# Attention scores from three 32-row terms per head, or from one 64-row and one 32-row matmul

## The chip, the cores and the metric

The kernel runs on one core of a Trainium2 chip. A core has five engines with queues of their own: TensorE (PE in the profile, with its weight loads listed as PEld), VectorE (DVE), ScalarE (ACT), GpSimd (POOL) and SyncE (SP), which here issues nearly all DMAs. Matmuls write to PSUM; the program uses it in banks of 128 x 512 float32. The metric is the device time of one execution in microseconds, and the number compared is the median of several runs.

## The reference

One transformer block with adaptive layer norm on 2048 tokens of width 448, in float32:

```python
mod = (silu(c) @ w_mod).reshape(1, 6, 1, -1)
sa, ca, ga, sb, cb, gb = (mod[:, i] for i in range(6))
h = layernorm(x) * (1 + ca) + sa
x = x + ga * A(h)          # softmax attention, 16 heads of 28, then @ wo
h = layernorm(x) * (1 + cb) + sb
x = x + gb * B(h)          # layernorm, 448 -> 1792, gelu, 1792 -> 448

# inside A, for each head
scores = einsum("bhqd,bhkd->bhqk", q, k) * 28 ** -0.5
p = softmax(scores)
o = einsum("bhqk,bhkd->bhqd", p, v)
```

The weights are drawn large, so that the scores are large too and the softmax needs the maximum of each row and scores of nearly float32 precision.

## The kernel before

**Precision.** Most matmuls run on `fp32r` operands. A value is split into a rounded part, hi, and the rest, lo, and a product is the sum of hi by hi, hi by lo and lo by hi. For scores this means three matmuls: K's hi by Q's hi, K's lo by Q's hi, K's hi by Q's lo.

**Stages.** In phase 1 (to about 181 us in the profiled execution) the kernel makes the first layer norm, Q, K and V for four blocks of 512 tokens, and some of the row maxima. `qk_task` (L336) makes four heads of Q or K for one block, in 128 rows: each head has 32, of which 28 are data. K has a one in row 28 of each head, and row 28 of Q's hi later gets minus the row maximum, so that the matmul subtracts it. `split` (L356) writes the hi and the lo part to DRAM, in `dscr[kind][part][g]`, for later. Attention follows (181 to 859 us), and then the MLP to the end at 1154 us. The MLP's weights are prepared in the last steps of attention.

**The attention loop** (L1017 to L1057) has 16 units, g by qt: four groups of four heads, by four blocks of 512 queries. A unit has 16 steps, one per 128 keys. A step makes the scores of four heads for 128 keys and 512 queries in two halves `hf` of two heads each. One half has a PSUM tile `s` of two banks (two such tiles take turns), filled by six matmuls: three terms by two heads, each on the 32 rows of its head (L1037 to L1040). Half 0 uses rows 0 to 63, half 1 rows 64 to 127. ScalarE takes the exponent of the half's 128 x 1024 scores (L1045) into `pt`. Behind the two halves stands PV of the step before (`av`, L1007): one matmul per head, 128 keys to 32 output rows, which the trace records as two passes each. In this text PV is the name of that block.

**The maxima.** The row maxima that group g + 1 needs are taken during group g, from hi parts alone. `max_one` (L395) is a 32-row matmul into one of three `mx` banks, followed by a reduction on VectorE (L397). `n_maxima` (L999) gives each step three or four, in turn, and few to those steps that also carry output projections; `emit_max` (L487) picks from the list of open maxima one whose head `j` suits the place: while half 0 computes, heads 2 and 3 (the other 64 rows), and heads 0 and 1 while half 1 does. TensorE works in the order in which the loop writes it, so a maximum that waits for its bank holds what is written behind it.

**Loads.** `load_q` (L571) reads the hi and lo of one unit's queries into slot `b0` or `b1`, in turn, as one tile of 128 x 2 x 512; `load_k` (L568) reads 512 keys into `a0` to `a3`. `load_hi` (L416) reads hi parts for the maxima. `max_fin` (L424) puts minus the maxima into Q's rows 28 of each head, in one DMA. `load_o` (L747) brings back staged attention outputs for the output projection (`t_wo`, L795). All these go through SP's queue in the order written. Slots are shared over the stages: the tags in `halved` (L67) are kept as two separate tiles of half the size, so that their halves can be used by different things.

The core of the score loop, before:

```python
for hf in range(2):
    s2 = ps_s2()
    for term, (kp, qp) in enumerate(((0, 0), (1, 0), (0, 1))):
        for jj in range(2):
            rows_ = slice(64 * hf + 32 * jj, 64 * hf + 32 * jj + 32)
            pe.matmul(s2[:, jj, :], ks[rows_, kp, kc], qs[rows_, qp, :], ...)
```

Of the kernel before, what the change touches and what calls it, by code (L numbers as in the profile page):

```python
# [14 lines left out]
F32R = mybir.dt.float32r  # L15
# [6 lines left out]
S = 2048  # L22
D = 448
H = 16
DH = 28
# [3 lines left out]
NB = S // 512  # L29
NG = H // 4  # L30
# [11 lines left out]
def tile_adaln_block(ctx: ExitStack, tc: tile.TileContext, x, wqkv, wo, w1, b1, w2, b2, c, w_mod, out):  # L42
    nc = tc.nc
    pe, act, dve, pool, sp = nc.tensor, nc.scalar, nc.vector, nc.gpsimd, nc.sync
# [6 lines left out]
    dr = ctx.enter_context(tc.tile_pool(name="dr", bufs=1, space=DRAM))  # L51
# [4 lines left out]
    def nm(t):  # L56
        uid[0] += 1
        return f"{t}_{uid[0]}"

    def sbt(tag, shape, dt=F32, bufs=1):  # L60
        return sb.tile(shape, dt, tag=tag, name=nm(tag), bufs=bufs)

    def slot(tag, shape, dt=F32R):
        return sb.tile(shape, dt, tag="slot_" + tag, name=nm("slot_" + tag), bufs=1)


    halved = ("a2", "a3", "b1")  # L67

    def slot4(tag, inner):
        if tag not in halved:  # L70
# [5 lines left out]
    def ps_s2():  # L76
        return psp[0].tile([128, 2, 512], F32, tag="s", name=nm("s"), bufs=psp[2])
# [4 lines left out]
    def ps_mx():  # L82
        return psp[0].tile([128, 512], F32, tag="mx", name=nm("mx"), bufs=psp[1])
# [7 lines left out]
    def f(t):  # L91
        return t.bitcast(F32)
# [184 lines left out]
    for k in range(NC):  # L277
        for j in range(2):
            pe.matmul(
                pm[32 * j : 32 * j + 32, :D], sil_b[:, k, :], wm_ac[k // 2][:, k % 2, j * D : (j + 1) * D],  # L280
                start=(k == 0), stop=(k == NC - 1),
# [21 lines left out]
    def v_init(i):  # L303
# [2 lines left out]


    dscr = [
        [[dr.tile([128, S], F32R, tag=f"d{kind}{part}{g}", name=f"d{kind}{part}{g}", bufs=1) for g in range(NG)] for part in range(2)]
        for kind in range(2)  # L310
    ]
    kh_sb = {}
# [16 lines left out]
    def qk_terms(b, kind, g):  # L329
        ts = terms448(  # L330
            *hT[b],
            lambda k: wq[kind][0](k)[:, 4 * g : 4 * g + 4, :], lambda k: wq[kind][1](k)[:, 4 * g : 4 * g + 4, :],
        )
        return ps_s(), [(w, h) for h, w in ts]

    def qk_task(b, kind, g, done=0, begun=None):  # L336
        p, ts = begun or qk_terms(b, kind, g)
        for i in range(done, len(ts)):
            pe.matmul(p, *ts[i], start=(i == 0), stop=(i == len(ts) - 1))  # L339
        emit_task(*p1_n)  # L340
        bias = ones_col if kind == 1 else zero_col
        if g == 0:
            tg = ("kh" if kind else "qh") + str(b)
            hi = sb.tile([128, 512], F32R, tag=tg, name=nm(tg), bufs=1)
            (kh_sb if kind else qh_sb)[(g, b)] = hi
        elif g == 1 and b < 2:

            hi = sbt("raw" if kind else "osb", [128, 512], F32R, bufs=3 if kind else 2)
            (kh_sb if kind else qh_sb)[(g, b)] = hi
        else:  # L350
            hi = sbt("hi", [128, 512], F32R, bufs=3)
        full = sbt("full", [128, 512], bufs=3)
        lo = sbt("lo", [128, 512], F32R, bufs=3)
        act.activation(full, p, AF.Identity, bias=bias)

        def split():  # L356
            (act.copy if b else dve.tensor_copy)(hi, full)
            if kind == 1 and (g, b) == (0, 1):
                k_diff.append(sbt("raw", [128, 512], F32R, bufs=3))
                pool.tensor_tensor(out=k_diff[0], in0=f(hi), in1=f(kh_sb[(0, 0)]), op=ALU.subtract)  # L360
            pool.tensor_tensor(out=lo, in0=full, in1=f(hi), op=ALU.subtract)
            sl = slice(b * 512, (b + 1) * 512)
            sp.dma_start(f(dscr[kind][0][g])[:, sl], f(hi))
            sp.dma_start(f(dscr[kind][1][g])[:, sl], f(lo))

        return split

# [13 lines left out]
    mxq = []  # L381
# [13 lines left out]
    def max_one(g, qt, cch, i, j, ps=None):  # L395
        m = max_mm(g, qt, i, j, kh_sb[(g, cch)], ps)
        dve.tensor_reduce(out=mxp[(g, qt)][:, i, j, cch : cch + 1], in_=m, op=ALU.max, axis=AX.X)  # L397
# [18 lines left out]
    def load_hi(kind, g, b):  # L416
        tg = ("kh" if kind else "qh") + str(b)
        t = sb.tile([128, 512], F32R, tag=tg, name=nm(tg), bufs=1)
        (kh_sb if kind else qh_sb)[(g, b)] = t
        sp.dma_start(f(t), f(dscr[kind][0][g])[:, b * 512 : (b + 1) * 512])  # L420

    late = []

    def max_fin(g, qt):  # L424
        m16 = sbt("m16", [128, 4, 4], bufs=2)
        c0 = 1 if (g, qt) in paired else 0
        dve.tensor_reduce(out=m16, in_=mxp[(g, qt)][:, :, :, c0:].rearrange("p i h c -> p h i c"), op=ALU.max, axis=AX.X)

        def put():
            p = ps_mx()  # L430
            pe.transpose(p[:16, :128], m16.rearrange("p h i -> p (h i)"), ident)
            r = sbt("full", [128, 512], F32R, bufs=3)[:16, :128]
            act.activation(r, p[:16, :128], AF.Copy, scale=-1.0)  # L433
            sp.dma_start(f(qst[g * NB + qt])[DH:128:32, 0, :].rearrange("j (i q) -> j i q", q=128), f(r))

        late.append([2, put, g * NB + qt])

# [47 lines left out]
    last_j = [None]  # L485

    def emit_max(n, half=None):  # L487
        for _ in range(n):
            if not mxq:
                return  # L490
            fits = [x for x, m in enumerate(mxq[:32]) if half is None or (m[4] // 2 == half and m[4] != last_j[0])]
            g, qt, cch, i, j = mxq.pop(fits[0] if fits else 0)
            last_j[0] = j
            max_one(g, qt, cch, i, j)
            count(g, qt, [cch])
# [27 lines left out]
    def finish_max(g, qt):  # L523
        while left[(g, qt)] > 0:
            emit_max(1)
# [33 lines left out]
    kst = {}  # L559
    qst = {}  # L560

    def load_parts(tag, kind, g, sl):
        t = slot(tag, [128, 2, 512])
        for part in range(2):
            sp.dma_start(f(t)[:, part, :], f(dscr[kind][part][g])[:, sl])
        return t

    def load_k(g, ch):  # L568
        kst[(g, ch)] = load_parts(f"a{ch}", 1, g, slice(ch * 512, (ch + 1) * 512))

    def load_q(u):  # L571
        g, qt = divmod(u, NB)
        qst[u] = load_parts(f"b{u % 2}", 0, g, slice(qt * 512, (qt + 1) * 512))

    b1_col = sbt("b1_col", [128, NFT])

# [167 lines left out]
    def last_g(qt):  # L744
        return NG - 2 if qt == NB - 1 else NG - 1

    def load_o(qt):  # L747
        for g, tag in zip(range(last_g(qt)), ("a2h", "a3h", "b1h")):
            t = slot(tag, [128, 2, 512])
            for part in range(2):  # L750
                sp.dma_start(f(t)[:, part, :], f(doh[part][g])[:, qt * 512 : (qt + 1) * 512])
            o_in[(qt, g)] = t
# [210 lines left out]
    q0, q1 = f"b{(NU - 2) % 2}", f"b{(NU - 1) % 2}"  # L963
# [53 lines left out]
    for u in range(NU):  # L1017
        g, qt = divmod(u, NB)
        for kt in range(NKT):
            step = u * NKT + kt  # L1020
            if kt == 1 and u + 1 < NU and u + 1 not in qst:
                load_q(u + 1)
            if kt == NKT - 6 and u + 1 < NU:
                finish_max(*divmod(u + 1, NB))
            tick_late()
            if not (three or mxq or late):
                three = True
                share(1, 3)
            pt = slot(ptags[step % 3], [128, 4, 512], F32)
            n = n_maxima(step)  # L1030
            n0 = 1 if n == 3 and step % 4 == 3 else 2

            ks, qs = kst[(g, kt // 4)], qst[u]
            kc = slice((kt % 4) * 128, (kt % 4 + 1) * 128)
            for hf in range(2):
                s2 = ps_s2()
                for term, (kp, qp) in enumerate(((0, 0), (1, 0), (0, 1))):  # L1037
                    for jj in range(2):
                        rows_ = slice(64 * hf + 32 * jj, 64 * hf + 32 * jj + 32)
                        pe.matmul(s2[:, jj, :], ks[rows_, kp, kc], qs[rows_, qp, :], start=(term == 0), stop=(term == 2))  # L1040
                    if hf == 0 and term < min(n0, n):
                        emit_max(1, 1)
                    if hf == 1 and ((term == 0 and n - n0 > 0) or (term == 2 and n - n0 > 1)):
                        emit_max(1, 0)
                act.activation(pt[:, 2 * hf : 2 * hf + 2, :], s2, AF.Exp, scale=SCALE)  # L1045
            if pend is not None:
                pu, pkt, pp, po = pend
                av(pu, pkt, pp, po)
                if pkt == NKT - 1:
                    end_unit(pu, po)  # L1050
            if kt == 0:
                o = ps_o()
            pend = (u, kt, pt, o)
            if qt == NB - 1 and kt % 4 == 3 and g + 1 < NG:
                load_k(g + 1, kt // 4)
            for fn in sched.pop(step, ()):
                fn()  # L1057
# [50 lines left out]
    for n in range(len(seq) + LAG):  # L1108
        if n < len(seq):
            b, i = seq[n]  # L1110
# [37 lines left out]
```

## Time and profile before

| | |
|---|---|
| median of three runs | 1153.68 us (1153.37 to 1156.09) |
| profiled execution, its time | 1156.12 us |
| profiled execution, its span | 1154.1 us |
| granted TensorE clock, mean | 0.997 |
| attention, first score matmul to last PV | 181.2 to about 859 us |
| a unit of attention (first twelve), PV to PV | 39.7 to 41.5 us |
| score matmuls (L1040) | 3072, mean 425 ns |
| maxima's matmuls (L392, `mx` from `kh`, `qh`) | 899, mean 471 ns |
| their reductions (L397) | 919, mean 684 ns |
| exponents (L1045) | 512, mean 1022 ns |
| PV matmuls (L1010) | 2048 in two passes each, mean 608 ns |

In the profile, a matmul's line gives its start, its duration and how many are merged in the line. Durations of matmuls overlap: the next one starts while the one before still has its tail, and matmuls on different rows of the array start together. What a matmul costs is therefore read from the distance between starts. An idle time in brackets is followed by what ended it.

### The profile page before, as it was taken

The page shows a single profiled execution, that of the slowest core. Times are in us where ns is not written, and L with a number is a line of the kernel's source. Part 1 is how long each engine was busy: PE and PEld are TensorE (multiplying, and loading weights), DVE is VectorE, ACT ScalarE, POOL GpSimd, SP SyncE. Part 2 cuts the span into 40 slices and gives each one's busy share as a digit, 9 for nine tenths or more (in the row PEclk, how much of TensorE's full clock was granted, in tenths as well). Part 3 has the DMA queues.
Part 4 walks back from the last instruction along what each step waited for, and adds up shares of the span by engine and source line. Part 5 has one row for each costly group of instructions (what it writes and reads, how often), then busy time and mean ns, then how long its engine had stood idle before and what let it go on. Part 6 is the DMA issues. An engine that isn't in the chain of part 4 may idle for free. (4 is left out here: it accounts for less than half of the span.)

```text
span 1154.1 us, 20722 instructions
## 1 busy us (share of the span) xinstructions
PE 1142.3 (99%) x8396; PEld 685.5 (59%) x8396; DVE 827.6 (72%) x1471; ACT 685.0 (59%) x855; POOL 215.0 (19%) x216
## 2 busy tenths in 40 slices
PE   8999999999999999999999999999999999999998
PEld 6767765444444444444444445555458888888887
DVE  6868787999888889889888976585448863444322
ACT  4666756877777787777777877675862221111110
POOL 2534431210000000000000011206213513213000
PEclk9999998999999999999999999999999999999999
DMA  8653354121132111321110321120323100000000
GB/s 299 206 145 114 100 193 119 38 65 57 31 96 79 57 38 38 88 71 55 50 57 29 83 84 44 41 78 8 110 69 90 48 33 1 1 32 1 32 1 32
DMA packets 50415, 81.07 MB, mean 70 GB/s; under 512 B 11512, under 2 KB 20812, under 8 KB 50320
## 3 DMA queue, kind: packets, MB, share of 16 engines
q1 hardware_dynamic: 49696, 79.01, 21.8%
q8 instruction: 66, 1.08, 0.4%
q10 hardware_dynamic: 288, 0.46, 0.1%
q0 software_dynamic: 336, 0.28, 0.1%
q14 instruction: 29, 0.24, 0.1%
HBM read 53.11 MB, written 26.35 MB: 69 GB/s over the span
## 5 line engine op out<-in xcount | busy, mean ns | idle before, releaser
L397 DVE TENSOR_REDUCE mxp<-mx 128x1 f32<-128x512 f32 x919 | 580.0, 684 | 112.8 <-PE mx L392 107.8
L1040 PE MATMUL s<-slot_b,slot_a 32*128 32x512 f32 x3072 | 384.1, 425 | 1.6 <-ACT full L433 0.7
L1045 ACT ACTIVATE slot_c<-s 128x1024 f32<-128x1024 f32 x342 | 331.7, 1022 | 87.4 <-PE s L1040 83.4
L1040 PEld LDWEIGHTS s<-slot_b,slot_a 32*128 32x128 f32 x3072 | 217.4, 184 | 239.7 <-ACT slot_c L1045 138.8
L392 PE MATMUL mx<-kh,qh 32*128 32x512 f32 x899 | 293.8, 471 | 0.4
L1045 ACT ACTIVATE slot_d<-s 128x1024 f32<-128x1024 f32 x170 | 164.8, 1021 | 44.7 <-PE s L1040 44.6
L1010 PE MATMUL o<-slot_c,v 128*32 128x512 f32 x1368 | 184.2, 608 | 0.4 <-ACT osb L979 0.4
L1081 ACT ACTIVATE full<-mx,b_col 128x512 f32<-128x512 f32 x56 | 38.5, 688 | 191.9 <-PE mx L317 179.8
L392 PEld LDWEIGHTS mx<-kh,qh 32*128 32x128 f32 x899 | 118.4, 182 | 13.3 <-DVE mxp L397 7.8
L1084 DVE CAST hi<-full 128x512 fp32r<-128x512 f32 x56 | 25.2, 450 | 135.0 <-ACT full L1081 135.0
L778 POOL TENSOR_TENSOR osb<-osb,osb 128x512 f32<-128x512 f32 x16 | 20.9, 1305 | 491.4 <-DMA osb<-drec 251.1
L1010 PE MATMUL o<-slot_d,v 128*32 128x512 f32 x680 | 90.6, 605 | 0.0
L1010 PEld LDWEIGHTS o<-slot_c,v 128*32 128x32 f32 x1368 | 27.2, 108 | 56.7 <-issue 52.0
L317 PE MATMUL mx<-y,slot_a 128*128 128x512 f32 x160 | 60.6, 395 | 0.0
L405 ACT ACTIVATE slot_d<-mx 128x512 f32<-128x512 f32 x48 | 27.0, 597 | 40.5 <-PE mx L392 40.3
L1085 DVE TENSOR_TENSOR lo<-full,hi 128x512 fp32r<-128x512 f32 x56 | 44.1, 788 | 5.6 <-DVE hi L1084 0.5
L317 PE MATMUL mx<-y,slot_c 128*128 128x512 f32 x152 | 47.5, 396 | 0.1
L1099 PE MATMUL s<-slot_v,lo 128*128 128x448 f32 x128 | 46.7, 365 | 0.0
L1097 PE MATMUL s<-slot_v,hi 128*128 128x448 f32 x128 | 46.6, 364 | 0.0
L317 PE MATMUL mx<-y,slot_v 128*128 128x512 f32 x112 | 39.2, 396 | 0.0
L317 PE MATMUL mx<-y,slot_b 128*128 128x512 f32 x112 | 39.0, 397 | 0.0
L339 PE MATMUL pa<-slot_c,slot_a 128*128 128x512 f32 x136 | 36.9, 405 | 0.0
(224 smaller groups left out, 1392.1 us busy)
## 6 DMA issues: line engine op xcount, KB each, us to landing
d<-lo SPq DMA_DIRECT2D x32, 256.0 KB
slot_b<-d SPq DMA_DIRECT2D x32, 256.0 KB
slot_a<-d SPq DMA_DIRECT2D x32, 256.0 KB
d<-hi SPq DMA_DIRECT2D x20, 256.0 KB
osb<-drec SPq DMA_DIRECT2D x15, 256.0 KB
out_dram<-xn SPq DMA_DIRECT2D x16, 224.0 KB
slot_v<-in_w_mod_dram SPq DMA_DIRECT2D x4, 784.0 KB
raw<-in_B_w_dram SPq DMA_DIRECT2D x14, 224.0 KB
```

Of the source, the lines that this page charges most:

```text
L317: pe.matmul(p, a, b, start=(i == 0), stop=(i == len(terms) - 1))
L339: pe.matmul(p, *ts[i], start=(i == 0), stop=(i == len(ts) - 1))
L392: pe.matmul(m, qh_sb[(g, qt)][js, i * 128 : (i + 1) * 128], k[js, :], start=True, stop=True)
L397: dve.tensor_reduce(out=mxp[(g, qt)][:, i, j, cch : cch + 1], in_=m, op=ALU.max, axis=AX.X)
L405: act.activation(r, m, AF.Relu)
L1010: pe.matmul(o[32 * j : 32 * j + 32, :], v_sb[kt // 4][:, kt % 4, 4 * g + j, :], p[:, j, :], start=(kt == 0), stop=(kt == NKT - 1),)
L1040: pe.matmul(s2[:, jj, :], ks[rows_, kp, kc], qs[rows_, qp, :], start=(term == 0), stop=(term == 2))
L1045: act.activation(pt[:, 2 * hf : 2 * hf + 2, :], s2, AF.Exp, scale=SCALE)
L1081: act.activation(gf, p, AF.Gelu_apprx_tanh, bias=b1_col[:, i : i + 1])
L1085: dve.tensor_tensor(out=glo, in0=gf, in1=f(ghi), op=ALU.subtract)
L1097: pe.matmul(pp, ghi[:, ts], w_hi, start=(m == 0), stop=False)
L1099: pe.matmul(pp, glo[:, ts], w_hi, start=False, stop=(m == NFT - 1))
```

## The change

Per half of a step, the six 32-row matmuls become four: two of 64 rows and two of 32. K's tile now holds, for each head, hi and lo one above the other in 64 rows, and Q's tile `q1` holds Q's hi twice, so one 64-row matmul gives K's hi by Q's hi plus K's lo by Q's hi. A second tile `q2` has Q's lo twice; a 32-row matmul adds K's hi by Q's lo. In each half the two heads now sit in rows 0 to 63 and 64 to 127. For half 0, K's hi lies in the upper 32 rows of each 64, for half 1 in the lower 32, so the 32-row matmuls of half 0 use row groups 0 and 2 and those of half 1 use row groups 1 and 3. The maxima of a half are written behind its four matmuls, and use the heads on the row groups that the 32-row matmuls leave free: odd heads in half 0, even heads in half 1. Their number per half stays.

To load the tiles in this form, K is stored with hi and lo exchanged for the lower 64 rows, in two DMAs where there was one, and is loaded in four DMAs for two; Q is loaded in six for two; K's hi for the maxima in two for one; minus the maxima are put in two for one. The tags `a1` and `b0` become halved, `q2` lives in `b0h` or `b1h`, and the third staged output moves from `b1h` to `a1h`.

```diff
-    halved = ("a2", "a3", "b1")
+    halved = ("a1", "a2", "a3", "b0", "b1")
...
     dscr = [
-        [[dr.tile([128, S], F32R, tag=f"d{kind}{part}{g}", name=f"d{kind}{part}{g}", bufs=1) for g in range(NG)] for part in range(2)]
+        [dr.tile([2, 128, S], F32R, tag=f"d{kind}{g}", name=f"d{kind}{g}", bufs=1) for g in range(NG)]
         for kind in range(2)
     ]
...
-            sp.dma_start(f(dscr[kind][0][g])[:, sl], f(hi))
-            sp.dma_start(f(dscr[kind][1][g])[:, sl], f(lo))
+            for part, src in enumerate((hi, lo)):
+                if kind == 0:
+                    sp.dma_start(f(dscr[0][g])[part, :, sl], f(src))
+                else:
+                    sp.dma_start(f(dscr[1][g])[part, 0:64, sl], f(src)[0:64])
+                    sp.dma_start(f(dscr[1][g])[1 - part, 64:128, sl], f(src)[64:128])
...
-        sp.dma_start(f(t), f(dscr[kind][0][g])[:, b * 512 : (b + 1) * 512])
+        sl = slice(b * 512, (b + 1) * 512)
+        if kind == 0:
+            sp.dma_start(f(t), f(dscr[0][g])[0, :, sl])
+        else:
+            sp.dma_start(f(t)[0:64], f(dscr[1][g])[0, 0:64, sl])
+            sp.dma_start(f(t)[64:128], f(dscr[1][g])[1, 64:128, sl])
...
-            sp.dma_start(f(qst[g * NB + qt])[DH:128:32, 0, :].rearrange("j (i q) -> j i q", q=128), f(r))
+            for hf in range(2):
+                sp.dma_start(
+                    f(qst[g * NB + qt][0])[32 * hf + DH : 128 : 64, hf, :].rearrange("j (i q) -> j i q", q=128),
+                    f(r)[8 * hf : 8 * hf + 8],
+                )
...
-            fits = [x for x, m in enumerate(mxq[:32]) if half is None or (m[4] // 2 == half and m[4] != last_j[0])]
+            fits = [x for x, m in enumerate(mxq[:32]) if half is None or (m[4] % 2 == half and m[4] != last_j[0])]
...
-    def load_parts(tag, kind, g, sl):
-        t = slot(tag, [128, 2, 512])
-        for part in range(2):
-            sp.dma_start(f(t)[:, part, :], f(dscr[kind][part][g])[:, sl])
-        return t
...
     def load_k(g, ch):
-        kst[(g, ch)] = load_parts(f"a{ch}", 1, g, slice(ch * 512, (ch + 1) * 512))
+        t = slot(f"a{ch}", [128, 2, 512])
+        src = f(dscr[1][g])[:, :, ch * 512 : (ch + 1) * 512]
+        for hf in range(2):
+            for jj in range(2):
+                h_ = 2 * hf + jj
+                sp.dma_start(f(t)[64 * jj : 64 * jj + 64, hf, :], src[:, 32 * h_ : 32 * h_ + 32])
+        kst[(g, ch)] = t

     def load_q(u):
         g, qt = divmod(u, NB)
-        qst[u] = load_parts(f"b{u % 2}", 0, g, slice(qt * 512, (qt + 1) * 512))
+        sl = slice(qt * 512, (qt + 1) * 512)
+        q1 = slot(f"b{u % 2}", [128, 2, 512])
+        q2 = slot(f"b{u % 2}h", [128, 512])
+        src = [f(dscr[0][g])[part, :, sl].rearrange("(y x r) n -> x y r n", y=2, r=32) for part in range(2)]
+        for jj in range(2):
+            rows_ = slice(64 * jj, 64 * jj + 64)
+            for hf in range(2):
+                sp.dma_start(f(q1)[rows_, hf, :], src[0][jj, hf][None].broadcast_to([2, 32, 512]))
+            sp.dma_start(f(q2)[rows_], src[1][jj])
+        qst[u] = (q1, q2)
...
-        for g, tag in zip(range(last_g(qt)), ("a2h", "a3h", "b1h")):
+        for g, tag in zip(range(last_g(qt)), ("a2h", "a3h", "a1h")):
...
-            ks, qs = kst[(g, kt // 4)], qst[u]
+            ks, (q1, q2) = kst[(g, kt // 4)], qst[u]
             kc = slice((kt % 4) * 128, (kt % 4 + 1) * 128)
             for hf in range(2):
                 s2 = ps_s2()
-                for term, (kp, qp) in enumerate(((0, 0), (1, 0), (0, 1))):
-                    for jj in range(2):
-                        rows_ = slice(64 * hf + 32 * jj, 64 * hf + 32 * jj + 32)
-                        pe.matmul(s2[:, jj, :], ks[rows_, kp, kc], qs[rows_, qp, :], start=(term == 0), stop=(term == 2))
-                    if hf == 0 and term < min(n0, n):
-                        emit_max(1, 1)
-                    if hf == 1 and ((term == 0 and n - n0 > 0) or (term == 2 and n - n0 > 1)):
-                        emit_max(1, 0)
+                for jj in range(2):
+                    r = slice(64 * jj, 64 * jj + 64)
+                    pe.matmul(s2[:, jj, :], ks[r, hf, kc], q1[r, hf, :], start=True, stop=False)
+                for jj in range(2):
+                    r = slice(64 * jj + 32 * hf, 64 * jj + 32 * hf + 32)
+                    pe.matmul(s2[:, jj, :], ks[r, hf, kc], q2[r, :], start=False, stop=True)
+                for _ in range(min(n0, n) if hf == 0 else max(n - n0, 0)):
+                    emit_max(1, 1 - hf)
                 act.activation(pt[:, 2 * hf : 2 * hf + 2, :], s2, AF.Exp, scale=SCALE)
```

## The prediction

> **What bounds the kernel now.** I read the page's busy line first, then the table by stretches, then the timeline of TensorE for two steps of attention. The page's line of busy time:
>
> ```profile
> PE 1142.3 (99%) x8396; PEld 685.5 (59%) x8396; DVE 827.6 (72%) x1471; ACT 685.0 (59%) x855; POOL 215.0 (19%) x216
> ```
>
> A stretch inside attention, the only stage whose matmuls change (the columns are PE, weight loads, DVE, ACT, POOL):
>
> ```profile
> 400.00:500.00 100.00, 100.00 (x946) 44.68 (x942) 89.16 (x148) 78.68 (x84) 7.68 (x6) 1.00 0.18 55
> ```
>
> PE is full, DVE nearly. PE's timeline through one step of four maxima, one of three (the step from 402.73), and the next one's start:
>
> ```profile
> 399.99 0.49 PE L1040 MATMUL s<-slot_b,slot_a 32*128 32x512 f32 x2
> 399.99 0.50 PE L392 MATMUL mx<-kh,qh 32*128 32x512 f32 x2
> 400.32 1.01 PE L1040 MATMUL s<-slot_b,slot_a 32*128 32x512 f32 x6
> 400.83 0.49 PE L392 MATMUL mx<-kh,qh 32*128 32x512 f32 x1
> 401.16 0.40 PE L1040 MATMUL s<-slot_b,slot_a 32*128 32x512 f32 x2
> 401.30 0.49 PE L392 MATMUL mx<-kh,qh 32*128 32x512 f32 x1
> 401.40 0.40 PE L1040 MATMUL s<-slot_b,slot_a 32*128 32x512 f32 x2
> 401.74 1.07 PE L1010 MATMUL o<-slot_c,v 128*32 128x512 f32 x8
> 402.73 0.50 PE L1040 MATMUL s<-slot_b,slot_a 32*128 32x512 f32 x2
> ```
>
> and the end of the second of these steps, with PV (L1010) and the next scores:
>
> ```profile
> 403.94 1.07 PE L1010 MATMUL o<-slot_d,v 128*32 128x512 f32 x8
> 404.94 0.50 PE L1040 MATMUL s<-slot_b,slot_a 32*128 32x512 f32 x2
> ```
>
> Starts tell more here than busy time. Matmuls on different row groups start together (two scores and two maxima at 399.99). A step lasts 2.74 us with four maxima, 2.21 with three, because there the two halves of a step use different rows and run side by side; with four, the second half waits for ScalarE to free its bank. A pair of steps is 4.95. In each, PV takes 1.00 (401.74 to 402.73).
>
> What a slot of PE costs, from the same timeline elsewhere. Matmuls of one shape, in a row:
>
> ```profile
> 131.34 1.36 PE L317 MATMUL pa<-slot_e,slot_b 128*128 128x448 f32 x6
> ```
>
> From 128 rows to 32 and on to PV, in a late step without maxima:
>
> ```profile
> 844.49 0.36 PE L317 MATMUL mx<-slot_e,lo 128*128 128x448 f32 x1
> 844.78 0.98 PE L1040 MATMUL s<-slot_b,slot_a 32*128 32x512 f32 x12
> 845.69 1.06 PE L1010 MATMUL o<-slot_c,v 128*32 128x512 f32 x8
> ```
>
> A maximum that starts alone, ahead of PV; transposes of 128 rows ahead of some of 64; and two reduces on VectorE:
>
> ```profile
> 234.75 0.49 PE L392 MATMUL mx<-kh,qh 32*128 32x512 f32 x1
> 235.17 0.64 PE L1010 MATMUL o<-slot_c,v 128*32 128x512 f32 x4
> ```
> ```profile
> 13.09 0.49 PE L240 MATMUL mx<-ident,xn 128*128 128x128 f32 x3
> 13.51 0.46 PE L292 MATMUL pa<-ident,full 64*128 64x64 f32 x4
> ```
> ```profile
> 400.56 1.29 DVE L397 TENSOR_REDUCE mxp<-mx 128x1 f32<-128x512 f32 x2 [0.33 <-PE mx L392]
> ```
>
> Matmuls of one shape follow each other every (1.36 - 0.36) / 5 = 0.20 us for 448 columns; for 512 it is 0.23 to 0.24 (the six scores from 400.32 start in pairs at 400.32, 400.56 and 400.83). From a 128-row matmul to a 32-row one the start comes 0.29 later (844.49 to 844.78): the change of shape costs 0.09. The first matmuls after it start with their weights not yet loaded and hold the next back to 0.33 (399.99 to 400.32), another 0.10. A slot with both, fresh weights and a change behind it, lasts 0.42 (234.75 to 235.17). 64 rows are no exception against 128: the last of three transposes (0.27 each) starts at 13.31 and the 64-row one at 13.51, 0.20 where the spacing is 0.11.
>
> **The change, part by part.**
>
> *Scores.* Per step twelve 32-row matmuls become four of 64 rows and four of 32. In rows' time a half becomes two slots: A (a pair of 64 rows), B (a pair of 32 rows with its maxima beside it); then C and D for the other half, then PV. The two halves can no longer run side by side, since each 64-row pair takes all 128 rows. The number of PE slots falls from six (three where halves overlap) to four, but each is followed by a change of shape: 64 to 32, 32 to 64, 64 to 32, 32 to PV. No row shows 64 against 32. Bounds: nothing (as between 32-row matmuls, 0.23 a slot; less is excluded, since 512 columns take that in every shape) and 0.19 (as between 128 and 32, 0.42 a slot). I take 0.42: 64 against 128 costs 0.09 in the rows above, so 64 rows are a shape of their own, and every change in this trace costs it. A step is then 4 x 0.42 + 1.00 = 2.68.
>
> The Trainium skill, page "TensorEngine Tiling (Array Packing)", section "Key Properties", says that a change of tiling mode drains TensorE, and lists 64-row and 32-row tilings as separate modes. By that rule the sum is the one taken here; the changes between 128 and 32 rows agree with it at 0.09 us.
>
> *Maxima.* The same reduces, at other places: two right behind B's pair, one or two behind D's. There are three mx banks. A bank comes back 1.31 us after its matmul with fresh weights: the first maximum starts at 399.99, its reduce at 400.56, and the fourth, in its bank, at 401.30. D begins 0.84 after B. So in a step of four the last maximum waits 1.31 - 0.84 = 0.47, and behind it on PE stand PV and the next scores, which ScalarE needs. Four-maxima steps: 2.68 + 0.47 = 3.15. In the next step the banks are free (the last reduce ends before its B): 2.68. A pair is 5.83, against 4.95: +0.88. VectorE needs 7 x 0.60 = 4.2 of it (two reduces span 1.29, one 0.69, so they start every 0.60), ScalarE four times 0.92: neither bounds. ScalarE's bank, which the second half waits for now, is free by then: each exp starts some 0.6 after its slot B or D and lasts 1.02, and the bank is wanted again a whole step after A or C. The program order has 112 steps of four and 112 of three: 112 x 0.88 = +98.5 us.
>
> *Steps with few maxima.* Ten steps beside the output projection have one or two: their scores took 1.25 (4.17 from PV to PV, less 1.00, less nine projection matmuls at 0.20 and a change), now 1.68: +4. In 22 steps without any they took 0.91 (844.78 to 845.69) to 1.14: +0.54 to +0.77 each, +15.
>
> *Loads, on SP's queue.* K's parts are stored and loaded in 4 pieces for 2, Q's loaded in 6 for 2, K's hi in 2 for 1, the maxima put in 2 for 1. An issue takes 0.32 to 0.55. Q for the next unit but one is issued as soon as its slot is free, a unit of 40 us before its use, and K a unit ahead, so these hide; if not, 4 more pieces and one more put would cost each unit 2.2 us, 33 in all. den's load stands behind one more put (0.55); its reciprocal rarely waits now and the longer steps give room: 0. Before attention there is no cover: kh's last loads are issued at 178.95, 2.2 us ahead of the first maximum at 181.17; eight more pieces ahead of them make up to 3.6. I take +3, between 0 and 4. Splitting two weight slots into halves moves no work: 0.
>
> *Sum.* 98.5 + 4 + 15 + 3 = +120. The profiled execution has a span of 1154.1 and a time of 1156.1, 2.4 above the median of 1153.7. On the median: 1274.
>
> **Rivals.**
>
> *The change costs nothing between 64 and 32 rows.* Slots 0.33, 0.23, 0.24, 0.32: a step of three is 2.12. But with four, D comes 0.47 after B and the bank back 1.21 after it (weights ready): 0.74 of waiting, 2.86. A pair is 4.98: +0.03 x 112 = 3, +2 in the other steps, +3 loads: 1162. Against it: every change seen costs something.
>
> *Half a change.* A drain of 0.09 with weights loaded ahead: slots 0.42, 0.32, 0.32, 0.32, wait 0.57, pair 5.33: +43 + 9 + 3, 1209. Or fresh weights without drain: 0.33 three times, 0.42, wait 0.64, pair 5.47: +58 + 11 + 3, 1226. For it: weights for rows in use are loaded ahead within one shape. The Trainium skill, page "TensorE: Matmul & The Clock Gate", Part 3, has weight loads overlap running matmuls only in other row groups; by it the second is the case without a drain. The trace disagrees within one shape: the second scores' weights load at 400.09, on the rows of matmuls begun at 399.99.
>
> *Faster: the count of PE slots decides.* If the change of shape is free and the last maximum in D finds its bank, a pair is 2 x 2.12 = 4.24, just over VectorE's 4.2: -0.71 x 112 = -80, +5, 1079. It turns on that one wait in D, 0.74 us in every second step, and decides only from a bank that is back 0.47 us after its matmul; the rows say 1.2 to 1.3.
>
> *The two 64-row matmuls run one after the other.* A and C become 0.65; the wait shrinks to 0.24; the pair is 6.52: +176 + 25 + 9 + 3, 1367. Against it: four 32-row ones and four 32-column ones start together.
>
> **How the numbers follow.** Forecast 0.68, with a range of its own from 1240 to 1300 (switch between 0.15 and 0.21, loads between 0 and 10). Half a change 0.10, no cost 0.08, faster 0.08, one after the other 0.06. Leaving out the last two and the forecast's own tails gives 1160 to 1305. A measurement here tells 0.3% (3.5 us) from no change. Faster: 0.08 and a quarter of the no-cost case, 0.10; within 0.3%: 0.03; slower: 0.87.
>
> **What will show it.** In the changed kernel's timeline: starts 0.42 apart from the 64-row pair to the 32-row pair and back (0.23 refutes the switch); both 64-row matmuls within 0.02 us; in steps of four the last maximum 0.47 after D's scores, waiting for VectorE; steps alternating 3.15 and 2.68; VectorE's share of a stretch near 76% (89 x 4.95 / 5.83), its idle time ended by TensorE; units of 47 us instead of 40; stages before and after attention unchanged. A free switch, or a D maximum without a wait, makes me wrong.

## The result and the profile after

The changed kernel takes 1513.38 us in the median (1500.69 to 1526.26), against 1153.64 before: a ratio of 1.3075, with a 95% interval of 1.2965 to 1.3186. The forecast was 1274, with a range up to 1305. The direction was right, and the size was three times too small. The profiled execution has a span of 1518.5 us and a mean granted clock of 0.898.

The page's line of busy time, after:

```profile
PE 1350.5 (89%) x7372; PEld 687.7 (45%) x7372; DVE 830.9 (55%) x1471; ACT 690.9 (45%) x855; POOL 214.8 (14%) x216
```

A stretch of 50 us inside attention, in the table by stretches (length, PE, weight loads, DVE, ACT, POOL, granted clock, DMA share, GB/s):

```profile
500.00:550.00 50.00, 43.78 (x260) 14.46 (x257) 29.15 (x48) 26.59 (x30) 1.27 (x1) 0.86 0.13 43
```

TensorE is no longer full: 88% here, at a clock of 0.86. VectorE, at 58%, is not the bound in its place. So something makes both wait. The step from 500.96 us, on PE's timeline, shows first what was forecast for the matmuls (L1064 is the 64-row pair, L1067 the 32-row pair, L396 the maxima, L1034 PV):

```profile
500.96 0.50 PE L1064 MATMUL s<-slot_b,slot_a 64*128 64x512 f32 x2
501.39 0.49 PE L1067 MATMUL s<-slot_b0h,slot_a 32*128 32x512 f32 x2
501.40 0.50 PE L396 MATMUL mx<-kh,qh 32*128 32x512 f32 x2
501.83 0.50 PE L1064 MATMUL s<-slot_b,slot_a 64*128 64x512 f32 x2
502.26 0.49 PE L1067 MATMUL s<-slot_b0h,slot_a 32*128 32x512 f32 x2
502.27 0.93 PE L396 MATMUL mx<-kh,qh 32*128 32x512 f32 x2
503.13 1.07 PE L1034 MATMUL o<-slot_c,v 128*32 128x512 f32 x8
504.12 0.50 PE L1064 MATMUL s<-slot_b,slot_a 64*128 64x512 f32 x2
```

Slots start 0.43 us apart. The last maximum waits: the two from 502.27 span 0.93 where one takes 0.49, so the second starts 0.44 after the first. The step lasts 3.16 us. Steps alternate 3.17 and 2.73, a pair 5.90, against 5.83 forecast. If that were all, the kernel would be near the forecast. It isn't all: once per unit one step takes 11 to 22 us, and up to four after it take 4 to 5. A unit takes 57 to 77 us instead of 40.

The waits say where. Of the changed kernel, two of the longest (engine, who is waited for: us in total, times, longest):

```profile
PEld mx L396 <- DVE mxp L401: 165.5, 127, 17.2
DVE rec L793 <- DMA den<-osb: 164.8, 15, 19.4
```

and of the kernel before, for the last of them:

```profile
DVE rec L769 <- DMA den<-osb: 5.7, 2, 4.7
```

`den` is the softmax denominator of a finished unit, loaded over SP's queue; its reciprocal stands in VectorE's order among the reductions of maxima. It now waits 15 times, 11 us on average and up to 19.4. One such stop, around 340 us, on SP, then VectorE, then TensorE (L595 and L596 load Q, L444 puts minus the maxima, L787 loads `den`):

```profile
336.74 1.21 SPq L595 DMA_DIRECT2D slot_b<-d  x1
337.99 3.06 SPq L596 DMA_DIRECT2D slot_b1h<-d  x1
348.12 3.13 SPq L444 DMA_DIRECT2D slot_b<-full  x2
351.30 0.59 SPq L787 DMA_DIRECT2D den<-osb  x1
```
```profile
342.71 2.48 DVE L401 TENSOR_REDUCE mxp<-mx 128x1 f32<-128x512 f32 x4 [0.84 <-PE mx L396]
354.03 0.25 DVE L793 RECIPROCAL rec<-den 128x16 f32<-128x16 f32 x1 [8.83 <-DMA den<-osb]
```
```profile
348.03 0.50 PE L1067 MATMUL s<-slot_b0h,slot_a 32*128 32x512 f32 x2
354.88 1.38 PE L396 MATMUL mx<-kh,qh 32*128 32x512 f32 x2 [6.35 <-DVE mxp L401]
356.19 0.79 PE L1064 MATMUL s<-slot_b,slot_a 64*128 64x512 f32 x2
```

The six DMAs of Q's tile are issued from 334.28 us on. SP cannot put the maxima into that tile before its loads have landed, at 348 and 351, and `den` stands behind the put. SP's own waits, over the whole run, name the tile's loads:

```profile
SPq L444 <- DMA slot_b<-d: 86.0, 21, 6.9
```

The reciprocal runs at 354.03. Until then VectorE reduces nothing, the three `mx` banks stay full, and the next maximum holds TensorE for 6.35 us. What follows runs at a lower clock, 0.79 us for a matmul of 0.50. The table by stretches, for the loads and for the end of the stop and the time behind it:

```profile
341.50:347.50 6.00, 6.00 (x43) 2.00 (x39) 2.86 (x5) 3.98 (x5) 0.00 (x0) 1.00 0.14 51
```
```profile
351.00:361.00 10.00, 6.12 (x24) 1.96 (x24) 4.69 (x9) 1.02 (x1) 0.00 (x0) 0.50 0.20 62
```

While nothing but Q's loads is under way, the DMA share is 0.14 of sixteen engines and they move 51 GB/s: 768 KB take 15 us. Before, Q's two loads of 256 KB were issued at 302.33 in the same unit, and the DMA engines were idle again from 306 on. The granted clock of the second stretch is 0.50; it falls at 350.8, 2.3 us into the stop, and is back at 1.00 from 361.0 on. Where a whole step falls into such a stretch, as from 414.77 on, behind the next stop, it takes 4.77 us instead of 2.73. The Trainium skill, page "TensorE: Matmul & The Clock Gate", Part 1, has the clock fall to half after an idle window of about 3.4 us; the half agrees, but here the clock was down before 3.4 us of the stop were over.

The loss lies in two places. Attention's first PV is at 211.8 us instead of 185.8 (+26.0), and from there to the last PV matmul's start it takes 1011.1 instead of 673.0 (+338.1). The MLP behind it takes some 295 us in both. Attention in the changed kernel, in the table by stretches:

```profile
211.80:1222.90 1011.10, 873.75 (x5088) 308.85 (x5086) 546.38 (x904) 519.57 (x559) 83.79 (x71) 0.86 0.14 45
```

TensorE is idle for 137 us of it (2 before); the rest of the +338 is longer steps, from the new matmuls and from the lower clock.

### The profile page after: what moved, and what is told of

Same layout as the page of the kernel before. It is cut to its first block, busy times and chain, and to the rows that moved or that the text cites. A ratio compares the mean times of both kernels' runs of the same rounds, so it can differ in the third digit from the quotient of the medians.

```text
span 1518.5 us, 18896 instructions
## 1 busy us (share of the span) xinstructions
PE 1350.5 (89%) x7372; PEld 687.7 (45%) x7372; DVE 830.9 (55%) x1471; ACT 690.9 (45%) x855; POOL 214.8 (14%) x216
## 5 line engine op out<-in xcount | busy, mean ns | idle before, releaser
L396 PE MATMUL mx<-kh,qh 32*128 32x512 f32 x899 | 323.2, 537 | 129.4 <-DVE mxp L401 129.3
L1064 PE MATMUL s<-slot_b,slot_a 64*128 64x512 f32 x1024 | 276.7, 537 | 1.3 <-ACT full L442 0.7
L1064 PEld LDWEIGHTS s<-slot_b,slot_a 64*128 64x128 f32 x1024 | 102.6, 197 | 293.9 <-ACT slot_c L1070 135.8
L1034 PE MATMUL o<-slot_c,v 128*32 128x512 f32 x1368 | 203.5, 669 | 0.0
L396 PEld LDWEIGHTS mx<-kh,qh 32*128 32x128 f32 x899 | 123.1, 198 | 165.7 <-DVE mxp L401 163.8
L1067 PE MATMUL s<-slot_b0h,slot_a 32*128 32x512 f32 x512 | 140.2, 544 | 0.0
L1067 PE MATMUL s<-slot_b1h,slot_a 32*128 32x512 f32 x512 | 134.8, 523 | 0.0
L1034 PE MATMUL o<-slot_d,v 128*32 128x512 f32 x680 | 101.0, 669 | 0.0
L793 DVE RECIPROCAL rec<-den 128x16 f32<-128x16 f32 x16 | 4.0, 253 | 164.8 <-DMA den<-osb 164.8
L1067 PEld LDWEIGHTS s<-slot_b0h,slot_a 32*128 32x128 f32 x512 | 51.6, 198 | 70.9 <-issue 70.9
L1067 PEld LDWEIGHTS s<-slot_b1h,slot_a 32*128 32x128 f32 x512 | 49.7, 191 | 67.5 <-issue 67.5
L1034 PEld LDWEIGHTS o<-slot_c,v 128*32 128x32 f32 x1368 | 28.2, 112 | 47.1 <-issue 46.5
```

Of the source, the lines that this page charges most:

```text
L396: pe.matmul(m, qh_sb[(g, qt)][js, i * 128 : (i + 1) * 128], k[js, :], start=True, stop=True)
L1034: pe.matmul(o[32 * j : 32 * j + 32, :], v_sb[kt // 4][:, kt % 4, 4 * g + j, :], p[:, j, :], start=(kt == 0), stop=(kt == NKT - 1),)
L1064: pe.matmul(s2[:, jj, :], ks[r, hf, kc], q1[r, hf, :], start=True, stop=False)
L1067: pe.matmul(s2[:, jj, :], ks[r, hf, kc], q2[r, :], start=False, stop=True)
```

## The experiments

The theory formed from the trace (A): a load whose source is two blocks of 32 rows, one DMA's outer dimension of two, runs on about two DMA engines; the loads are late, `den` lands behind them, and VectorE and TensorE stop. Rivals: the number of DMAs on SP's queue (B), or the new matmuls and the clock themselves (C).

**Plain loads.** Q and K of the changed kernel loaded by DMAs of 32 plain rows; more of them.

```diff
-                sp.dma_start(f(t)[64 * jj : 64 * jj + 64, hf, :], src[:, 32 * h_ : 32 * h_ + 32])
+                for p_ in range(2):
+                    sp.dma_start(f(t)[64 * jj + 32 * p_ : 64 * jj + 32 * p_ + 32, hf, :], src[p_, 32 * h_ : 32 * h_ + 32])
...
-                sp.dma_start(f(q1)[rows_, hf, :], src[0][jj, hf][None].broadcast_to([2, 32, 512]))
-            sp.dma_start(f(q2)[rows_], src[1][jj])
+                h_ = 2 * hf + jj
+                for p_ in range(2):
+                    sp.dma_start(f(q1)[64 * jj + 32 * p_ : 64 * jj + 32 * p_ + 32, hf, :], src[0, 32 * h_ : 32 * h_ + 32])
+                sp.dma_start(f(q2)[64 * jj + 32 * hf : 64 * jj + 32 * hf + 32], src[1, 32 * h_ : 32 * h_ + 32])
```

> The changed kernel with Q's and K's tiles loaded by plain DMAs of 32 rows each (12 per Q tile, 8 per piece of K) in place of DMAs whose source is two blocks of 32 rows (6 and 4). The matmuls, the maxima and their order stay. Theory A (the loads in two-block form move on few DMA engines at about 50 GB/s, den's load lands behind them, the reciprocal holds VectorE, the mx banks stay full and TensorE stops for 11 to 21 us in each unit): the stalls go although there are more DMAs, pairs of steps stay at 5.90 us, granted clock back to about 1.00, time 1270 to 1310 us. Theory B (the number of DMAs on SP's queue makes the stalls): at least as slow as the changed kernel, 1500 us or more. Theory C (the stalls come from the new matmul order or from the granted clock): about 1510 us, unchanged.

Measured: 1284.27 us, a ratio to before of 1.1119 (1.1089 to 1.1150). Most units take 47.4 us, three of the first twelve 48 to 52; the first PV is at 189.0; the pair is 5.90. The stretch from 500 to 600 us, and what is left of the wait:

```profile
500.00:600.00 100.00, 99.91 (x659) 34.07 (x660) 75.04 (x123) 66.94 (x72) 6.22 (x5) 1.00 0.21 62
```
```profile
DVE rec L795 <- DMA den<-osb: 13.8, 4, 7.3
```

In this stretch TensorE is full again, VectorE at 75%, the clock at 1.00. Behind one of the waits that are left, which leaves TensorE idle for 0.90 us, the clock is low all the same:

```profile
395.00:401.50 6.50, 6.50 (x33) 1.91 (x25) 2.71 (x5) 2.26 (x3) 1.27 (x1) 0.50 0.25 72
```

So 229 of the 360 us lost belong to the form of the loads, and neither to their number (B) nor to the matmuls (C). Of the 229, 23 us are the start. In attention, which is 210 us shorter than in the changed kernel, TensorE is idle for 2 us instead of 137, so some 135 us were stops and some 75 longer steps, mostly by the low clock behind them. The other 130 are the matmuls and the maxima's bank, nearly as forecast, and some 10 us of what is left of waits and low clock.

**`den` by another queue.** The slow loads stay; the denominators go over GpSimd's queue.

```diff
-            q_ = pool if u == NU - 1 else sp
+            q_ = pool
```

> The changed kernel with its slow loads, but the DMAs of the denominators (den, drec, the broadcast back) are issued from GpSimd's queue in every unit, as before only in the last. Theory A (den behind the loads is what stops VectorE): reciprocals no longer wait, the stops in each unit fall from 11 us or more to under 2 us, and only the late start of attention (about 25 us) and the longer steps stay: 1290 to 1340 us. If TensorE stops for Q's tile itself or for minus the maxima, the time stays at 1450 us or more.

Measured: 1343.24 us (ratio 1.1624, 1.1589 to 1.1659), 3 above the expected upper end, and 170 less than with `den` on SP. The reciprocal's wait falls from 164.8 to 10.5 us:

```profile
DVE rec L793 <- DMA den<-osb: 10.5, 8, 7.9
```

So it is `den` behind the loads that stopped VectorE. Of what stays above the plain loads, the late start is 22 us (first PV at 211.4). The rest has several causes. In unit 0, where K's loads are still being issued until 227 us, the output projection's weights come late and VectorE's copy of them waits:

```profile
243.09 0.62 DVE L752 CAST slot_e<-full 128x448 fp32r<-128x448 f32 x1 [10.57 <-POOL full L749]
```

The first stop of the changed kernel, in unit 0, has this cause too, and not `den`: there the copy waits 14.6 us. In one later unit TensorE waits 4.7 us for staged outputs (`slot_a2h<-o`), and in four it is idle for 0.9 to 1.3 us while VectorE waits for outputs that need `osb<-drec`, which is now on GpSimd's queue.

**The kernel before, with four added loads per unit.** Its scores stay; in ten units, 4 x 128 KB are also loaded into a tile that nothing reads, in two-block form, in plain form, or as four blocks of 16 rows, each of every fourth row (the three lines `src = ...`, of which each kernel has one).

```diff
+        if 2 <= u < 12:
+            t3 = slot("b1h", [128, 2, 512])
+            for part in range(2):
+                src = f(dscr[0][part][g])[:, sl].rearrange("(y x r) n -> x y r n", y=2, r=32)
+                src = f(dscr[0][part][g])[:, sl].rearrange("(x y) n -> x y n", y=64)
+                src = f(dscr[0][part][g])[:, sl].rearrange("(j r x) n -> j x r n", j=2, x=4)
+                for jj in range(2):
+                    sp.dma_start(f(t3)[64 * jj : 64 * jj + 64, part, :], src[jj])
```

> The kernel before, with its own scores and loads, and in ten units four added loads of 128 KB in the two-block form behind Q's loads, into a tile that nothing reads. Theory A: some 10 us of loads at 50 GB/s stand ahead of den; VectorE waits some 3 to 8 us in each of the ten units, and the clock drops behind it: 1175 to 1260 us. Theory C (the stalls belong to the new matmuls): 1154 us, within 3 us.

> The same four added loads of the same bytes in the kernel before, as plain blocks of 64 rows. Theory A (the form counts, neither bytes nor the number of DMAs): within 3 us of 1154 us. Theory B (bytes or number): the same loss as with the two-block loads.

> The kernel before with the four added loads of 128 KB again, now as four blocks of 16 rows each instead of two of 32. If a load is spread over as many DMA engines as its source has blocks, these move at about 100 GB/s with a DMA share of about 0.25, the added loads take 5 us in place of 10, and most of the 78 us goes: 1154 to 1175 us. If any source in blocks is slow alike, 1232 us as with two blocks.

Measured: 1232.52 us with two blocks (ratio 1.0679, 1.0650 to 1.0707), 1154.02 with plain rows (0.9995, 0.9986 to 1.0004), 1170.82 with four blocks (1.0151, 1.0112 to 1.0191). The reciprocal's wait in each, in that order:

```profile
DVE rec L776 <- DMA den<-osb: 68.9, 11, 8.6
```
```profile
DVE rec L776 <- DMA den<-osb: 5.6, 2, 4.4
```
```profile
DVE rec L776 <- DMA den<-osb: 22.2, 11, 4.8
```

and the DMA share and rate while the added loads run, with two blocks, with plain rows and with four:

```profile
272.00:274.00 2.00, 2.00 (x24) 1.07 (x24) 1.50 (x4) 1.65 (x4) 0.00 (x0) 1.00 0.13 50
```
```profile
264.00:265.00 1.00, 1.00 (x16) 0.38 (x11) 1.00 (x2) 1.00 (x2) 0.00 (x0) 1.00 0.95 344
```
```profile
270.00:271.00 1.00, 1.00 (x15) 0.67 (x10) 0.71 (x2) 0.51 (x2) 0.00 (x0) 1.00 0.27 104
```

Bytes, DMA count and slots are the same in all three, and the 40 added issues take 22 to 24 us in each; only the rows' grouping differs. With the old matmuls, two blocks alone cost 78 us, 7.8 a unit. The share is about 2 and 4 sixteenths and the rate 50 and 104 GB/s: as many engines as blocks. The Trainium skill, page "DMA: Bandwidth & Descriptors", section "Why a DMA increments its semaphore by 16 and not by 1", states it as a rule: the number of DMA engines is the largest up to 16 that divides the outermost dimension of both sides. The three shares agree (for 64 plain rows it gives 16).

The added loads go into a tile of their own, so the put does not wait for them. `den` is issued soon and is late all the same, in the run with two blocks:

```profile
274.57 0.56 SPq L770 DMA_DIRECT2D den<-osb  x1
283.51 0.25 DVE L776 RECIPROCAL rec<-den 128x16 f32<-128x16 f32 x1 [5.81 <-DMA den<-osb]
```

In all ten units with added loads the reciprocal runs 8.4 to 9.2 us after `den` is issued, against 1.3 to 4.1 in the kernel before. So slow loads hold `den` in two ways: through the put, which keeps SP from issuing it, and on the queue itself. In the changed kernel the first holds in most units; in four the reciprocal comes 9.5 to 10.8 us after an issue.

**All scores on 64 rows.** On the plain loads, Q's lo is padded with zeros to 64 rows, so that only maxima have 32.

```diff
-                    r = slice(64 * jj + 32 * hf, 64 * jj + 32 * hf + 32)
-                    pe.matmul(s2[:, jj, :], ks[r, hf, kc], q2[r, :], start=False, stop=True)
+                    r = slice(64 * jj, 64 * jj + 64)
+                    pe.matmul(s2[:, jj, :], ks[r, hf, kc], q2[r, hf, :], start=False, stop=True)
```

> The plain-load version with Q's lo padded with zeros to 64 rows, so that all eight score matmuls of a step have 64 rows and only the maxima have 32. Theory (each change between 64 and 32 rows costs a drain of 0.09 us and fresh weights of 0.10, 0.19 together): in steps without maxima three of the five changes go and a step falls from 2.71 us to 2.1 to 2.3, while in steps with maxima the maxima no longer lie beside scores: slots 0.33, 0.32, 0.42, twice, and 1.00 for PV, 3.14, and 3.3 to 3.4 with four maxima (the bank comes back 1.31 after its matmul, the second group of maxima starts 1.07 after the first); 1330 to 1350 us. Rival (the 0.42 us of a slot belong to the 64-row matmuls themselves, not to the change of shape): steps without maxima stay at 2.7 us.

Measured: 1331.00 us (ratio 1.1532, 1.1510 to 1.1554). A step without maxima takes 2.12 us instead of 2.71, and its four slots lie 0.34, 0.23, 0.24 and 0.31 apart:

```profile
1004.65 0.50 PE L1067 MATMUL s<-slot_b,slot_a 64*128 64x512 f32 x2
1004.99 0.39 PE L1070 MATMUL s<-slot_b1h,slot_a 64*128 64x512 f32 x2
1005.22 0.40 PE L1067 MATMUL s<-slot_b,slot_a 64*128 64x512 f32 x2
1005.46 0.39 PE L1070 MATMUL s<-slot_b1h,slot_a 64*128 64x512 f32 x2
1005.77 1.07 PE L1037 MATMUL o<-slot_c,v 128*32 128x512 f32 x8
```

So 64 rows cost what 32 do, and three changes between the two cost 2.71 - 2.12 = 0.59, 0.20 each. With maxima in slots of their own the steps are 3.36 and 3.16, a pair 6.52:

```profile
404.39 0.50 PE L1067 MATMUL s<-slot_b,slot_a 64*128 64x512 f32 x2
404.73 0.40 PE L1070 MATMUL s<-slot_b0h,slot_a 64*128 64x512 f32 x2
405.05 0.50 PE L396 MATMUL mx<-kh,qh 32*128 32x512 f32 x2
405.48 0.50 PE L1067 MATMUL s<-slot_b,slot_a 64*128 64x512 f32 x2
405.82 0.40 PE L1070 MATMUL s<-slot_b0h,slot_a 64*128 64x512 f32 x2
406.14 0.68 PE L396 MATMUL mx<-kh,qh 32*128 32x512 f32 x2
```

The second group of maxima starts 1.09 after the first instead of 0.87, and the last one's wait falls from 0.44 to 0.68 - 0.49 = 0.19. That is the bank's 1.3 us seen from two distances. A step with maxima has five changes of shape in either version, but six slots here instead of four: without the maxima's place beside the 32-row matmuls a pair is 0.62 slower.

## Why the prediction was right in direction and wrong in size

- **Change of shape between 64 and 32 rows, taken as 0.19 us, a slot as 0.42.** Right: 0.20 and 0.43. The rule of the Trainium skill that the prediction set beside it (a change of tiling mode drains) agrees between 64 and 32 rows too; how the 0.20 divides into drain and fresh weights was not measured. Within one shape weights are loaded ahead even on rows in use: the slots of 0.23 and 0.24 above follow each other on all 128 rows. The page "TensorE: Matmul & The Clock Gate" of the Trainium skill, Part 3, lists weight loads as overlapping only with matmuls on other rows; here the measurement decides against it.
- **The last maximum's wait, taken as 0.47.** Right: 0.44. The pair was 5.90 for 5.83. Most units of the plain-load version are 7.0 to 7.5 us longer than before, and eight pairs at 0.88 are 7.0. The 10 us by which this version (1284) lies above 1274 are mostly in three other units (0, 4 and 8), which are 8.3 to 11.8 us longer: a wait for `den` in two, a clock of 0.50 in two.
- **Both 64-row matmuls side by side; steps without maxima; the sum for the matmuls.** Right: they start within 0.01 us; such a step takes 2.71 for 2.68. The version with plain loads is 130 us slower than before, where +120 was the whole sum.
- **"K's parts are stored and loaded in 4 pieces for 2, Q's loaded in 6 for 2 [...] so these hide."** Wrong, and this is the step that failed. The pieces were counted and priced by their issue (0.32 to 0.55 us); their transfer was taken to be as fast as before's. It is 15 us for a Q tile. The cover, a unit of 40 us, was long enough for Q itself, which TensorE never waited for in the stop shown. It was not there for what stands behind Q on the same queue.
- **"den's load stands behind one more put [...]: 0."** Wrong with it. The put must wait for the tile's loads, `den` for the put (in some units for the queue alone), VectorE's next reductions for `den`'s reciprocal, TensorE for the banks. The bound of 33 us, 2.2 a unit, was worked out from issues alone; the form of the loads cost 229.
- **"+3, between 0 and 4" for the start.** Right for plain loads (3.2), 26 with the slow ones.
- **The clock** was not in the sum. In the changed kernel it falls to 0.50 at each of the long stops, 2 to 4 us after the stop begins. TensorE's waits of 0.4 us a step leave it at 1.00 (the stretch from 500 to 600 us with plain loads). But it needs no long stop: in the same run it was 0.50 from 395.0 to 401.8 us, where TensorE's longest idle time had been 0.90 us. What makes it fall there stays open.
- The rivals with a cheaper or a free change, and the one with the 64-row matmuls in sequence, are refuted by the 0.43 us slots and the equal starts. None of the rivals was about the loads.

A row of before could have warned. The broadcast of the reciprocals, `osb<-drec`, has a source of four rows repeated, four blocks again, and in the list of issues it lands later than the small transfers of the same queue (operation, size, us from issue to landing):

```profile
osb<-drec POOLq DMA_DIRECT2D x1, 256.0 KB, 5.5
...
den<-osb POOLq DMA_DIRECT2D x1, 8.0 KB, 2.4
drec<-rec POOLq DMA_DIRECT2D x1, 8.0 KB, 2.8
```

256 KB in the 2.7 to 3.1 us beyond those are 85 to 97 GB/s, near the 104 of four blocks. Two plain loads of Q together, twice the bytes, were through in under 3.7 us from the first one's issue. Over SP's queue the kernel before shows the rate itself, in the unit where this DMA is issued at 233.84:

```profile
236.00:237.00 1.00, 1.00 (x17) 0.81 (x15) 0.75 (x2) 0.43 (x1) 0.00 (x0) 1.00 0.26 100
```

A share of 0.26 and 100 GB/s are those of four blocks.

## What to carry to other kernels

Price a DMA by its shape as well as its bytes and its issue: an outermost dimension of 2 or 4 gave 50 or 104 GB/s here, where plain rows reached 344 and cost nothing that could be seen. When a load gets slower, look past its own consumer at what is queued behind it, here a small load that the busiest reducer needs. On TensorE count the changes of row shape beside the slots: a step had two before and has five now. At 0.2 us each, the three new ones cost 0.6 us, more than the two slots of 0.23 that four fewer matmuls can save.

## What the runs showed that was not expected

- The rate of a DMA followed the number of blocks of its source: 0.13 of sixteen engines and 50 GB/s for two, 0.27 and 104 GB/s for four, 0.95 and 344 GB/s for plain rows. Whether the source's or the destination's outermost dimension decides was not separated; the destination was 64 plain rows in each of the three.
- SP's issue slows with the transfer when several such loads are outstanding: from 0.5 us for an early DMA of a Q tile to 3.06 us for its last (337.99), so later DMAs of other data start late too.
- One stop of TensorE of 6.35 us goes with 10 us at a granted clock of 0.50, 6 of them behind the stop. The two steps around it take 15.25 us instead of 5.90 (PV at 346.61 to PV at 361.86): 6.35 us of the stop and 3.0 us of low clock. A wait in the wrong place is paid nearly one and a half times.
